# Splitting new expert weights on VectorE alone, over four points of a slot

## The chip, the cores and the metric

The kernel runs on one core of a Trainium2 chip. The metric is the device time in microseconds; several executions of one kernel are given by their median.

## The reference

Three stages follow one another on 10,112 tokens (2 sequences of 5,056) of 256 channels:

```python
h = a_t[:, t] * h + norm * sig_i * x          # gated linear scan over time, fp32
logits = x @ w_gate + modality_bias[modality_id]; e = argmax(logits)
out[e] = gate * (relu(x[e] @ w1[e]) @ w2[e])  # 8 experts, 256 -> 1024 -> 256
...                                           # and the same again, without the bias
```

The scan's output is the tokens' input of the first mixture of experts, whose output is that of the second. Only the expert with the highest logit works on a token, so which expert's weights are needed is known only at run time.

## The kernel before, in words

**Work.** The scan runs in 10 chunks of up to 512 time steps (`chunk_at`), whose rows are scattered by expert into the DRAM table X1. The experts' work is cut into slots of T = 256 tokens of one expert: 40 slots of the first layer and 40 of the second are always run (`slots`), and more, under a condition, where the tokens are spread badly. Which expert a slot has, and whether its weights differ from those that its weight set holds, a planner on VectorE works out from the counts (`plan_steps`); the engines read it into registers.

**Precision.** Each fp32 value v is split into a high part h, written by ScalarE in the type float32r, and a low part l = v - h. A product is then three TensorE products: hh, hl and lh (L911 to L913 for the first product, L925 to L927 for the second).

**A slot.** It has POINTS = 6 points. At points 0 to 3, `ffn1` does a quarter of the hidden units each: 12 products, then hTh by ScalarE (L915) and hTl by VectorE (L916). Three PSUM buffers (`ph`) hold the quarters, so TensorE can run ahead of VectorE by that much. At points 4 and 5, `ffn2` does half of the second product each (24 products); the first half needs the hidden quarters 0 and 1, the second half quarters 2 and 3. At point 3 the next slot's rows are transposed (`transposes`, xh by ScalarE, xl by VectorE). The end of a slot's work (`end_steps`: output rows by L937, L942 and L956, and in the first layer the choice of expert and the row's place for the second layer, L347 to L380 and L958 to L964, then GpSimd's scatter, L218) is spread over the points of the next slot.

**Weights.** There are two weight sets, used by slots in turn (`wset`), each of w1h, w1l, w2h and w2l. `load_weights` has SyncE fetch the next slot but one's weights in quarters of 128x1024 into `stage` buffers (five of them): part 0 is two quarters of w1, part 1 two quarters of w2. In the main loop both are put on a list at point 4 and taken from it one per point, so at points 4 and 5, if the slot's plan is due by then. `split` turns quarters of `stage` into high and low parts: `piece` has ScalarE write h (L874) and then the engine named by a letter in `by` write l (L875), V for VectorE and G for GpSimd. In the main loop the quarters 0 and 1 of the next slot are split at point 4, 2 and 3 at point 5 (`SPLIT`), with `by` = 'VVGG': the low parts of w1 on VectorE, those of w2 on GpSimd. Part 4 of `split` is a small extra piece of 128x64 in the first layer, the gate columns of the second layer's choice (`stagew`), on VectorE. The very first slot has its quarters split before the main loop, with 'VVVG'. All of it stands under a branch on the register f2 (L791), which skips it where the weights are already there. `own_gates` (L851) stands behind quarter 1 under a further branch (L855).

**Order.** Each engine runs its instructions in program order. The order is written out by hand: an agenda of ticks (`at`, `at_all`, `early`, `later`) lays the scan's steps, the planner's and the end steps between the points. GpSimd has the scatters, some copies of a few columns, and the w2 pieces. Between the layers `nest` (L1076) holds the conditional slots of the first layer behind a branch that every engine takes.

Of the kernel before, what the change touches and what calls it, by code (L numbers as in the profile page):

```python
# [29 lines left out]
CUTS = (1, 2, 3, 4, 6, 8)  # L30
SW_QUEUES = 8
POINTS = 6
SPLIT = (4, 4, 5, 5)
AHEAD = 11
T0 = 45
START = (5, 15, 34)
# [29 lines left out]
         send=32)]  # L66
LISTS = (4, 4, 4, 4, 8)
LATE = 4
BY = ('VVVG', 'VVGG', 'VVGG')
WARM = ((0, 'r', 1, 4, 2), (0, 'i', 1, 8, 2), (0, 'q', 1, 10, 3))  # L70
ALIGN = (0, 5)

# [1 line left out]
def STEP(c):  # L74
    return STEPS[min(c, len(STEPS) - 1)]
# [104 lines left out]
def scan_moe_moe2(tc, xT, rT, iT, apar, mod, mbias, wg1, wg2, wA1, wB1, wA2, cst_d, ids_d, tab_d, out):  # L180
# [11 lines left out]
    with ExitStack() as st:  # L192
# [130 lines left out]
        def run(steps):  # L323
            for f in steps:
                f()
# [67 lines left out]
        def at(tick, f, early=False):  # L393

            agenda.setdefault(tick, ([], [], []))[0 if early else 1].append(f)
# [301 lines left out]
        def fresh(pi):  # L697

            return pi == 0 or plans[pi][0] != plans[pi - 1][0]
# [2 lines left out]
        main = [(pi, s) for pi, pl in enumerate(plans) for s in range(pl[3])]  # L702
        NS = len(main)
        xT_, hT, pos = {}, {}, {}

        class Ring:

# [3 lines left out]
            def __init__(self, pool_, shape, dt, name, n):  # L711
                self.args, self.n, self.at_hand = (pool_, shape, dt, name), n, []
# [26 lines left out]
        class Slot:  # L739


            def __init__(self, pi, s, ws, pool_, bufs, tag=""):
                self.pi, self.s, self.ws, self.pool, self.bufs, self.tag = pi, s, ws, pool_, bufs, tag
                self.layer = plans[pi][0]
                self.always = not tag and s < 2 and fresh(pi)
                self.maybe = s >= plans[pi][3]
                self.v = None
                self.xpool, self.xtag = pool_, tag
                self.tiles = {}

# [28 lines left out]
        def guard(sl):  # L779

            if not sl.maybe:
                return nullcontext()
            if sl.v is None:
                sl.v = sl.entry(2, {ET.SP, ET.Activation, ET.DVE, ET.PE, ET.Pool}, 1)
            return tc.If(sl.v > 0)

        def when(slot, f, body):
            if slot.always:
                body()
            else:  # L790
                with tc.If(f > 0):  # L791
                    body()
# [9 lines left out]
        def load_weights(sl, part, gates=True):  # L802
            wA = wA1 if sl.layer == 1 else wA2
            if part == 0:
                sl.ev = sl.entry(0, {ET.SP}, E - 1)
                sl.f = None if sl.always else sl.entry(1, {ET.SP}, 1)
            js = {0: (0, 1), 1: (2, 3), 2: ()}[part]
            for j in js:
                sl.t(f"st{j}")
            gates_too = part > 0 and gates and sl.layer == 1  # L810
            if gates_too:
                sl.t("stw")

            def body():
                w = wA[bass.ds(sl.ev, 1)]
                for j in js:
                    SP.dma_start(sl.t(f"st{j}")[:], w[:, :, j * F:(j + 1) * F].rearrange("o p f -> p (o f)"))
                if gates_too:
                    SP.dma_start(sl.t("stw")[:], wg_all[:, bass.ds(sl.ev, 1)].rearrange("p o c d -> p (o c) d"))

            when(sl, sl.f, body)
# [25 lines left out]
        def first_gate(sl):  # L847
            gate(sl.gw, [sl.ring(n_).next()[:] for n_ in ("pt", "ph")], sl.t("stw"))
            SP.dma_start(wg_all[:, bass.ds(sl.ev, 1)].rearrange("p o c d -> p (o c) d"), sl.t("stw")[:])
# [15 lines left out]
                            V.tensor_reduce(out=stw[:, i * 4:i * 4 + 4, half * 4 + e], in_=t4, axis=AX.X, op=ALU.add)  # L865
                SP.dma_start(wg_all[:, bass.ds(ev, 1)].rearrange("p o c d -> p (o c) d"), stw[:])

        def split(sl, *parts, by=BY[2]):

            h1, l1, h2, l2 = wset[sl.ws]  # L870
            eng = dict(V=V, G=G)

            def piece(h, l, src, by=V):
                A.activation(h, src, func=ACTF.Copy)  # L874
                by.tensor_tensor(out=l, in0=src, in1=h.bitcast(F32), op=ALU.subtract)  # L875

            def body():
                for part in parts:
                    if part == 4:
                        continue  # L880
                    src = sl.t(f"st{part}")[:]
                    if part < 2:
                        piece(h1[:, part, :], l1[:, part, :], src, eng[by[part]])
                    else:
                        c = slice(part * 4 - 8, part * 4 - 4)
                        piece(h2[:, c, :D], l2[:, c, :D], src.rearrange("p (c d) -> p c d", d=D), eng[by[part]])
                if 1 in parts and sl.layer == 1 and not sl.always:
                    own_gates(sl)
                if 4 in parts and sl.layer == 1:
                    piece(h2[:, :, D:], l2[:, :, D:], sl.t("stw")[:])  # L890

            if 0 in parts and not sl.always:
                sl.f2 = sl.entry(1, {ET.Activation, ET.DVE, ET.Pool} | ({ET.SP} if sl.layer == 1 else set()), 1)
            when(sl, None if sl.always else sl.f2, body)

# [71 lines left out]
        slots = [Slot(pi, s, t % 2, mp, (3, 5)) for t, (pi, s) in enumerate(main)]  # L967
# [10 lines left out]
        for pi in range(1, len(plans)):  # L978
            layer, after, _, _, _, t0 = plans[pi]
            if layer == 1:  # L980
                by = slot_tick(t0 - 2, 3) - STEP(after - 1)["send"] - plan_ticks(pi)
# [34 lines left out]
        def early(upto):  # L1016

            later(upto - 1)
            if ticks[0] < upto:
                a, b, c = agenda.get(upto - 1, none)  # L1020
                run(a)
                agenda[upto - 1] = [], b, c

        def later(upto, *others):

            while ticks[0] < upto:
                a, b, c = agenda.pop(ticks[0], none)
                ticks[0] += 1
                run(a)
                for l in [f() for f in c] + list(others if ticks[0] == upto else ()):  # L1030
                    b = weave(b, l)
                run(b)
                others = others if ticks[0] < upto else ()
            for l in others:
                run(l)
# [8 lines left out]
        for sl in slots[:2]:  # L1044
            sl.ev = sl.entry(0, {ET.SP}, E - 1)
            first_gate_load(sl)
        load_weights(slots[1], 0)
        for i, tick in enumerate(FIRST):
            at(tick, lambda i=i: split(slots[0], i, by=BY[0]), early=True)
        later(T0)  # L1050
        load_weights(slots[1], 1, gates=False)
        transposes(slots[0])
# [66 lines left out]
        ends = [Slot(pi2, s, (NS + i) % 2, mp, (3, 5)) for i, s in enumerate(range(plans[pi2][3], plans[pi2][2]))]  # L1119
        line = slots + ends  # L1120
        prev = nest = None
        todo = []
        for t, sl in enumerate(slots):
            nxt, nx2 = (line[t + 1:] + [None, None])[:2]
            last1 = plans[sl.pi][0] == 1 and plans[sl.pi][4]
            a, b, c_, d, e, f = end_steps(prev)
            tick = lambda point: slot_tick(t, point) + 1
            run(a)
            if nest and sl.layer == 2:
                nest()  # L1130
                nest = None
            for point in range(POINTS):
                early(tick(point))
                if point < 4:
                    ffn1(sl, point)
                else:
                    ffn2(sl, point - 4)
                if last1 and sl.s == plans[sl.pi][3] - 2 and point == 2:
                    later(sent(NC - 1) + 1)
                    fetch, nest = maybe_steps(sl.pi)  # L1140
                    fetch()
                if t == 0 and point == 0:
                    for k in range(KD):
                        SP.dma_start(wgr[:, k, :], wg2[:, k, :].rearrange("p e -> e p"))
                if t == 0 and point in GATE:
                    first_gate(line[GATE.index(point)])
                    split(line[GATE.index(point)], 4)
                if nxt and point == 3:
                    with guard(nxt):
                        transposes(nxt)  # L1150
                if nxt:
                    parts = [i for i in range(4) if SPLIT[i] == point]
                    if parts:
                        split(nxt, *parts, *([4] if 3 in parts and t else []), by=BY[1 if t == 0 else 2])
                if nx2 and point == 4:
                    todo += [(nx2, lambda sl=nx2: (load_rows(sl), load_weights(sl, 0))), (nx2, lambda sl=nx2: load_weights(sl, 1))]
                if point == 2:
                    while todo:
                        later(listed[todo[0][0].pi] + 1)
                        todo.pop(0)[1]()  # L1160
                if todo and listed[todo[0][0].pi] < tick(point):
                    todo.pop(0)[1]()
                if point == 4:
                    run(e)
                later(tick(point), *{0: [b], 1: [c_], 2: [d], 5: [f]}.get(point, []))
            prev = sl
# [52 lines left out]
```

## Time and profile before

| | us |
|---|---|
| median of 3 executions | 1195.64 |
| lowest, highest | 1190.05, 1197.01 |
| the profiled execution's own time | 1185.72 |
| its span (first to last instruction) | 1183.9 |
| TensorE busy | 1090.3 (92%) |
| VectorE busy | 670.7 (57%) |
| ScalarE busy | 511.6 (43%) |
| GpSimd busy | 384.7 (32%) |

The rows below come from one profiled execution, and their times count from its span's start. An instruction's row gives start, duration, engine, source line, operation, output and inputs, and in brackets the idle time of its engine before it with what ended it. Engine names: PE is TensorE, DVE VectorE, ACT ScalarE, POOL GpSimd, SP SyncE; a q behind a name is the engine's sequencer. PEclk is the granted TensorE clock as a share of full speed, with 1.0 for 2.4 GHz and 0.5 for 1.2 GHz.

### The profile page before, as it was taken

Reading aid. Unit: us, or ns where it says so; the run is one execution under the profiler, and the core shown is the slowest. Engines: PE = TensorE matmul, PEld = TensorE weight load, DVE = VectorE, ACT = ScalarE, POOL = GpSimd, SP = SyncE. Lnnn points to the kernel's source line nnn. Section 1 sums busy time; section 2 is a strip of 40 time slices with the busy share of each in tenths; the row PEclk is TensorE's granted clock in tenths of the full one; section 3 lists DMA queues with packets and bytes.
Section 4 is the critical chain, followed back from the end, with each engine's and each line's share of the span. In section 5 each row is a group of like instructions: output and inputs, shape, how many; then the busy total and the mean of one; then the engine's idle time right before and its main releaser. Section 6 shows DMA issues by size and latency. Waiting matters only on the chain. (4 is left out here: it accounts for less than half of the span.)

```text
span 1183.9 us, 27134 instructions
## 1 busy us (share of the span) xinstructions
PE 1090.3 (92%) x9112; PEld 1069.1 (90%) x9112; DVE 670.7 (57%) x1945; ACT 511.6 (43%) x817; POOL 384.7 (32%) x414
## 2 busy tenths in 40 slices
PE   4287899887999999999999899999999999999997
PEld 2286899877999899999999899999999999999997
DVE  6786798768776867565456734333434443333352
ACT  7744576437263734223334323322534542224362
POOL 2425352356242514241212411311333531113152
PEclk9698999989899999999999899999999999999999
DMA  7766554355333212151115233113332431113350
GB/s 243 242 138 237 167 184 149 112 184 177 109 109 114 100 47 74 38 150 47 45 48 155 93 94 117 46 46 116 116 114 80 133 117 50 42 54 105 121 177 26
DMA packets 71305, 133.70 MB, mean 113 GB/s; under 512 B 11804, under 2 KB 39459, under 8 KB 71106
## 3 DMA queue, kind: packets, MB, share of 16 engines
q1 hardware_dynamic: 59250, 100.20, 27.9%
q0 software_dynamic: 11856, 31.25, 7.4%
q8 instruction: 76, 1.25, 0.5%
q14 instruction: 123, 1.01, 0.3%
HBM read 95.49 MB, written 37.04 MB: 112 GB/s over the span
## 5 line engine op out<-in xcount | busy, mean ns | idle before, releaser
L911 PE MATMUL ph<-xh,w1h 128*128 128x256 f32 x1312 | 376.0, 287 | 28.3 <-DVE base L377 6.5
L925 PE MATMUL po<-w2h,hTh 128*128 128x256 f32 (+1 forms) x1344 | 392.6, 292 | 4.0 <-issue 2.2
L927 PE MATMUL po<-w2h,hTl 128*128 128x256 f32 (+1 forms) x1344 | 382.3, 284 | 4.8 <-DVE hTl L916 2.5
L926 PE MATMUL po<-w2l,hTh 128*128 128x256 f32 (+1 forms) x1344 | 381.6, 284 | 3.0 <-issue 1.9
L912 PE MATMUL ph<-xl,w1h 128*128 128x256 f32 x1312 | 370.7, 283 | 4.4 <-DVE xl L902 4.4
L913 PE MATMUL ph<-xh,w1l 128*128 128x256 f32 x1312 | 371.0, 283 | 2.0 <-DVEq L855 1.0
L916 DVE SCALAR_TENSOR_TENSOR hTl<-ph,hTh 128x512 fp32r<-128x512 f32 x336 | 231.3, 688 | 235.0 <-ACT hTh L915 178.2
L915 ACT ACTIVATE hTh<-ph 128x512 fp32r<-128x512 f32 x336 | 199.2, 597 | 346.4 <-PE ph L913 283.1
L911 PEld LDWEIGHTS ph<-xh,w1h 128*128 128x128 f32 x1312 | 253.1, 193 | 31.4 <-issue 13.8
L925 PEld LDWEIGHTS po<-w2h,hTh 128*128 128x128 f32 x1344 | 255.6, 190 | 6.3 <-issue 3.7
L927 PEld LDWEIGHTS po<-w2h,hTl 128*128 128x128 f32 x1344 | 254.9, 190 | 6.9 <-DVE hTl L916 4.2
L926 PEld LDWEIGHTS po<-w2l,hTh 128*128 128x128 f32 x1344 | 255.4, 190 | 4.3 <-issue 3.0
L912 PEld LDWEIGHTS ph<-xl,w1h 128*128 128x128 f32 x1312 | 251.1, 191 | 4.6 <-DVE xl L902 4.6
L913 PEld LDWEIGHTS ph<-xh,w1l 128*128 128x128 f32 x1312 | 250.5, 191 | 2.9 <-DVEq L855 1.4
L218 POOL DMA_INDIRECT out_dram<-orow,xr x88 | 86.6, 984 | 284.1 <-ACT orow L937 237.8
L937 ACT ACTIVATE orow<-po,xr 128x256 f32<-128x256 f32 x124 | 57.7, 472 | 239.0 <-PE po L927 229.8
L218 POOL DMA_INDIRECT X<-orow,rib x80 | 80.8, 1010 | 179.7 <-DVE lgb L956 47.8
L875 POOL TENSOR_TENSOR w2l<-stage,w2h 128x1024 fp32r<-128x1024 f32 x37 | 94.2, 2566 | 132.2 <-ACT w2h L874 132.2
L942 DVE TENSOR_SCALAR orow<-po,xr 128x256 f32<-128x256 f32 x44 | 21.3, 483 | 148.7 <-PE po L927 148.7
L218 POOL DMA_INDIRECT X<-row,ria x79 | 90.1, 1141 | 24.1 <-issue 19.4
L460 PE MATMUL ps<-wI,it 128*128 128x136 f32 x280 | 49.3, 302 | 21.4 <-DVE it L439 15.6
L460 PEld LDWEIGHTS ps<-wI,it 128*128 128x128 f32 x280 | 40.0, 201 | 24.2 <-ACT rt L412 11.1
(171 smaller groups left out, 1042.1 us busy)
## 6 DMA issues: line engine op xcount, KB each, us to landing
stage<-in_wA SPq DMA_DIRECT2D x76, 512.0 KB
xr<-X SPq DMA_DIRECT2D x84, 258.0 KB
rt<-in_rT SPq DMA_DIRECT2D x18, 512.0 KB
it<-in_iT SPq DMA_DIRECT2D x18, 512.0 KB
xt<-in_xT SPq DMA_DIRECT2D x18, 512.0 KB
X<-zr SPq DMA_DIRECT2D x17, 258.0 KB
it<-in_wB SPq DMA_DIRECT2D x4, 512.0 KB
out_dram<-orow,xr POOLq DMA_INDIRECT x88
```

The lines of the kernel that those rows point to most:

```text
L218: i = G.indirect_dma_start(out=dst, out_offset=bass.IndirectOffsetOnAxis(ap=idx, axis=0), in_=rows, in_offset=None, bounds_check=bound, oo ...
L460: PE.matmul(p[:, k * (P + E):(k + 1) * (P + E)], l[:, k, :], wI[:, k, :], start=True, stop=True)
L875: by.tensor_tensor(out=l, in0=src, in1=h.bitcast(F32), op=ALU.subtract)
L911: PE.matmul(p[:, j, :], h1[:, k, cs], sl.t("xh")[:, k, :], start=k == 0, stop=False)
L912: PE.matmul(p[:, j, :], h1[:, k, cs], sl.t("xl")[:, k, :], start=False, stop=False)
L913: PE.matmul(p[:, j, :], l1[:, k, cs], sl.t("xh")[:, k, :], start=False, stop=k == KD - 1)
L915: A.activation(hh[:], p[:], func=ACTF.Relu)
L916: V.scalar_tensor_tensor(out=hl[:], in0=p[:], scalar=0.0, in1=hh[:].bitcast(F32), op0=ALU.max, op1=ALU.subtract)
L925: PE.matmul(p[h][:, :wd], hh, h2[:, c, :wd], start=c == 0, stop=False)
L926: PE.matmul(p[h][:, :wd], hh, l2[:, c, :wd], start=False, stop=False)
L927: PE.matmul(p[h][:, :wd], hl, h2[:, c, :wd], start=False, stop=c == KF - 1)
L937: A.activation(orow[:, h, :D], p[h][:, :D], func=ACTF.Copy, scale=g1[:, h:h + 1])
```

## The change

The letter sets `BY` go; `split` defaults to 'VVVV', so that in the main loop and in the conditional slots every low part is VectorE's. Only the first slot keeps 'VVVG'. The four quarters of the next slot are split at points 2, 3, 4 and 5, one each, if they were requested at least LOADED = 4 points before; otherwise at the old points. The moment of the request is kept per slot in `came`. The register f2 is read at the first `split` of a slot, whichever part that has.

```diff
-SPLIT = (4, 4, 5, 5)
+SPLIT = (2, 3, 4, 5)
+SPLIT_LATE = (4, 4, 5, 5)
+LOADED = 4
...
-BY = ('VVVG', 'VVGG', 'VVGG')
...
+        now = [-POINTS]
...
-                self.v = None
+                self.v = self.f2 = None
...
                 sl.f = None if sl.always else sl.entry(1, {ET.SP}, 1)
+                sl.came = {}
+            sl.came[part] = now[0]
...
-        def split(sl, *parts, by=BY[2]):
+        def split(sl, *parts, by='VVVV'):
...
-            if 0 in parts and not sl.always:
+            if sl.f2 is None and not sl.always:
                 sl.f2 = sl.entry(1, {ET.Activation, ET.DVE, ET.Pool} | ({ET.SP} if sl.layer == 1 else set()), 1)
...
-            at(tick, lambda i=i: split(slots[0], i, by=BY[0]), early=True)
+            at(tick, lambda i=i: split(slots[0], i, by='VVVG'), early=True)
...
+        now[0] = 0
...
             for point in range(POINTS):
+                now[0] = t * POINTS + point
...
                 if nxt:
-                    parts = [i for i in range(4) if SPLIT[i] == point]
+                    when_ = lambda i: SPLIT[i] if t * POINTS + SPLIT[i] >= nxt.came.get(i // 2, 1 << 20) + LOADED else SPLIT_LATE[i]
+                    parts = [i for i in range(4) if when_(i) == point]
                     if parts:
-                        split(nxt, *parts, *([4] if 3 in parts and t else []), by=BY[1 if t == 0 else 2])
+                        split(nxt, *parts, *([4] if 3 in parts and t else []))
```

## Rows read from the trace of the kernel before

**Rows 1.** The page's part 1: busy us (share of the span) and instructions by engine.

```profile
PE 1090.3 (92%) x9112; PEld 1069.1 (90%) x9112; DVE 670.7 (57%) x1945; ACT 511.6 (43%) x817; POOL 384.7 (32%) x414
```

**Rows 2.** Busy time by stage: two stretches.

```profile
core 0: us, PE busy (x) PEld busy (x) DVE busy (x) ACT busy (x) POOL busy (x), PEclk, DMA share, GB/s
...
149.00:255.00 106.00, 95.34 (x770) 90.98 (x769) 83.92 (x311) 57.27 (x84) 43.04 (x60) 0.95 0.49 156
...
700.00:1165.00 465.00, 465.00 (x3958) 465.00 (x3957) 178.21 (x259) 173.54 (x281) 132.44 (x101) 1.00 0.30 93
```

**Rows 3.** The timeline of TensorE: instructions behind gaps.

```profile
91.48 0.58 PE L911 MATMUL ph<-xh,w1h 128*128 128x256 f32 x1 [5.67 <-DVE db L348]
...
113.58 0.73 PE L460 MATMUL ps<-wI,it 128*128 128x136 f32 x4 [3.19 <-ACT row L470]
...
146.20 0.58 PE L911 MATMUL ph<-xh,w1h 128*128 128x256 f32 x1 [3.20 <-DVE cnt L563]
...
284.98 0.39 PE L927 MATMUL po<-w2h,hTl 128*128 128x264 f32 x1 [0.89 <-DVE hTl L916]
...
298.82 0.55 PE L911 MATMUL ph<-xh,w1h 128*128 128x256 f32 x1 [6.19 <-DVE base L377]
...
656.68 0.55 PE L911 MATMUL ph<-xh,w1h 128*128 128x256 f32 x1 [6.35 <-DVEq L1076]
```

**Rows 4.** The timelines of GpSimd and VectorE beside pieces of w2, and undisturbed.

```profile
106.86 4.98 POOL L875 TENSOR_TENSOR w2l<-stage,w2h 128x1024 fp32r<-128x1024 f32 x2 [5.79 <-ACT w2h L874]
...
109.81 2.06 DVE L379 TENSOR_TENSOR pbb<-pbb,ohb 128x16 f32<-128x16 f32 x1
...
353.98 0.17 DVE L379 TENSOR_TENSOR pbb<-pbb,ohb 128x16 f32<-128x16 f32 x1
...
83.29 2.48 DVE L586 TENSOR_TENSOR big<-av,tab 1x64 f32<-1x64 f32 x1
...
671.12 2.10 DVE L964 TENSOR_TENSOR rib<-rb,vbb 128x2 int32<-128x2 f32 x1
```

**Rows 5.** Line 875: instructions, duration in ns (least/median/most), first and last start.

```profile
L875 DVE TENSOR_TENSOR w1l<-stage,w1h x38: 1198/1220/1227, 47.1 to 1150.7; 128x1024 fp32r<-128x1024 f32 x38
L875 POOL TENSOR_TENSOR w2l<-stage,w2h x37: 2353/2552/2953, 63.4 to 1154.1; 128x1024 fp32r<-128x1024 f32 x37
```

**Rows 6.** The waits of TensorE: us in total, times, longest.

```profile
PE ph L911 <- ACTq L791: 1.7, 2, 0.9
...
PE po L926 <- DVE w2l L875: 1.0, 1, 1.0
PE ph L913 <- DVEq L855: 1.0, 2, 0.5
PE ph L913 <- DVE w1l L875: 1.0, 2, 0.8
...
PE ph L911 <- ACT w1h L874: 0.6, 1, 0.6
```

**Rows 7.** The timeline of ScalarE, and busy time by stage from 92 us.

```profile
96.57 1.06 ACT L412 ACTIVATE rt<-rt 128x1024 f32<-128x1024 f32 x1 [5.50 <-DMA rt<-in_rT]
...
92.00:104.00 12.00, 10.96 (x67) 10.07 (x66) 5.18 (x30) 6.13 (x9) 6.80 (x10) 0.78 1.02 399
```

**Rows 8.** Lines 1076 and 791, sequencers: ns (least/median/most), first and last start.

```profile
L1076 ACTq EVENT_SEMAPHORE  x2: 17/17/17, 653.1 to 653.2; - x2
L1076 DVEq EVENT_SEMAPHORE  x2: 21/21/21, 656.5 to 656.6; - x2
...
L1076 DVEq COMPARE_BRANCH  x1: 56/56/56, 653.5 to 653.5; - x1
...
L791 DVEq COMPARE_BRANCH  x188: 43/56/69, 103.7 to 1173.4; - x188
```

**Rows 9.** The timelines of VectorE and ScalarE in a slot of the second layer.

```profile
736.69 0.69 DVE L916 SCALAR_TENSOR_TENSOR hTl<-ph,hTh 128x512 fp32r<-128x512 f32 x1 [0.73 <-ACT hTh L915]
...
740.82 0.48 ACT L937 ACTIVATE orow<-po,xr 128x256 f32<-128x256 f32 x1
```

**Rows 10.** Busy time by stage, 115 to 120 us.

```profile
115.00:120.00 5.00, 5.00 (x35) 5.00 (x34) 3.48 (x16) 1.36 (x3) 1.14 (x5) 0.73 0.54 152
```

## The prediction

> **What bounds the kernel now.** I read the page's engine line first, then busy times by stage, then the gaps on TensorE one by one. TensorE is busy for 1090.3 of 1183.9 us [rows 1]. By stage it is full from 700 to 1165 us (465.00 of 465.00), where the second layer runs, and VectorE is busy there for only 38% [rows 2]. No change to the splitting can gain in that stretch; it can only lose. Between 149 and 255 us TensorE has 95.34 of 106 us and VectorE 83.92 [rows 2]: two engines near their limit, tied by a program order written out by hand. So the gain has to come out of TensorE's gaps before 700 us.
>
> The gaps have a pattern. In the first layer (and at the step to the second) the long ones come some 9 to 11 us after pieces of new weights: 5.67 us before 91.48, 3.19 before 113.58, 3.20 before 146.20, 6.19 before 298.82, 6.35 before 656.68 [rows 3]. Each time TensorE did the first two or three quarters of the next slot's first product and then ran out, because VectorE was late: the first four end on work that VectorE does or passes on, the fifth on VectorE's queue at L1076.
>
> Why is VectorE late? GpSimd's two pieces w2l<-stage take about 2.5 us each. While one of them runs, the next VectorE `tensor_tensor` with two SBUF inputs does not end before it does. At 106.86 GpSimd begins 4.98 us of pieces; VectorE's L379, which takes 0.17 us undisturbed (353.98), takes 2.06 us from 109.81, and ends (111.87) when GpSimd does (111.84) [rows 4]. Fourteen VectorE instructions are stretched so beside pieces that the change moves, two at each of seven switches; the first is at 83.29, the last at 671.12 [rows 4]. Their time over that of undisturbed ones is 4.2, 3.3, 3.0, 3.0, 4.3, 3.8 and 3.9 us by switch, 25.5 us in all. VectorE pays more for GpSimd's help than the help saves it.
>
> **The change, part by part.** *The engine.* GpSimd has 37 such pieces of 2.55 us, VectorE 38 of 1.22 us [rows 5]. One on GpSimd belongs to the first slot, whose call keeps 'VVVG'; 36 move, two at each of 18 switches: 7 up to 668 us, 11 later. VectorE gets 2 x 1.22 = 2.44 us more per switch and loses the stall. Even if nothing of the 2.44 is hidden, the first seven switches come out at 25.5 - 7 x 2.44 = 8.4 us less VectorE time.
>
> *The places.* Weights of the next slot but one are requested at points 4 and 5 of a slot; I followed the loop with its due times through all 80 slots, and none of the requests is late, so the new condition always picks (2, 3, 4, 5) and never the late set. The two w1 pieces go from point 4 to 2 and 3; the w2 pieces are then alone at 4 and 5. Per gap, the low end is the stall less 2.44, the high end the whole gap. As VectorE has idle time before the gaps (22 of 106 us in 149 to 255 [rows 2]), I take half of the 2.44 as hidden:
> - 113.58: stall 3.3, less 1.22: 2.0 (0.8 to 3.2).
> - 146.20: 3.0 less 1.22: 1.8 (0.6 to 3.2).
> - 298.82: 4.3 less 1.22: 3.1 (1.9 to 6.2).
> - 91.48: 4.2 less 1.22 is 3.0, but the piece at point 2 now stands ahead of the first slot's gate piece, for which TensorE already waits 1.0 us [rows 6]: minus 1.2; and ScalarE waits for a scan input until 96.57 whatever TensorE does, while the DMA share is 1.02 [rows 7]. I take 1.0 (-1.2 to 3.0).
> - 656.68: this gap ends when VectorE comes through the skipped branch of L1076: it reaches the branch at 653.5 and is out at 656.5. ScalarE was out at 653.1, so at most 3.3 us can go [rows 8]. The stall is 3.8, less 2.44 is 1.4; I take 1.6, since the w1 pieces start earlier (0 to 3.3).
>
> For this last term the Trainium skill (SBUF — State Buffer, "Who interferes with whom") says that whichever of VectorE with two SBUF inputs and a GpSimd instruction that reads SBUF starts first holds the shared ports for the whole instruction. It agrees with the 2.06 us, and speaks against the change too: an added 1.22 us piece could hold up a scatter before the branch; by that this term would be 0.4 and the sum 1.2 us smaller.
>
> *Waits that go.* TensorE waits five times at a slot's start for fresh w1 (1.0 + 1.0 + 0.6 us) [rows 6]; those pieces come two points earlier: 2.6 gained (0 to 2.6). Twice it waits for ScalarE's branch (1.7 us) [rows 6], which now comes earlier: 1.0 (0 to 1.7).
>
> *Costs.* The piece at point 2 stands ahead of hTl of the last quarter on VectorE, and of hTh on ScalarE with its copy. At 284.98 TensorE waits 0.89 for hTl already [rows 3]: minus 1.2 there (0 to -2.4). In the second layer hTl of the last quarter comes at 736.69 to 737.38 [rows 9]; 1.22 later is 738.6. The half product that needs it begins near 739.4: its first output is read at 740.82 [rows 9], after 12 products of 0.12 us (1090.3 / 9112 [rows 1]). It is hidden, by 0.8 us: that cover is thin. Two more branches per slot cost VectorE 0.056 us each [rows 8]; over 40 slots of the first layer 4.5 us beside an engine that is not always the bound: minus 0.7 (0 to -4.5). GpSimd's 36 x 2.55 = 92 us fall away, but only scatters stand behind them: 0.
>
> *The clock.* After the gap at 113.58 the granted clock is 0.73 in 115 to 120 [rows 10], a stretch at the 1.2 GHz level in place of 2.4: 5 x 0.27 = 1.35 us lost. Likewise after 146.20. If both gaps nearly close, 2.5 comes back (0 to 2.7).
>
> Sum: 2.0 + 1.8 + 3.1 + 1.0 + 1.6 + 2.6 + 1.0 - 1.2 - 0.7 + 2.5 = 13.7 us. The profiled execution took 1185.72 (span 1183.9 and 1.8 around it), so 1172.0 in its terms. It lies 9.9 below the median shown, 1195.64; the prediction for a median is 1195.64 - 13.7 = 1181.9, about 1182. Of itself this case may lie between 1176 and 1189.
>
> **The rivals.** *The gaps fill again.* Before 250 us something else is late next: the scan's inputs (DMA share 1.02 in 92 to 104 [rows 7]), or VectorE, at 79% between 149 and 255. Then only the later terms stay: 3.1 + 1.6 + 1.9 (three of the five w1 waits) + 1.0 - 1.2 - 0.7 = 5.7 us, 1190. For it: the order is fixed by hand, and slack gained early is easily spent. Against: every early gap here ends on VectorE's chain.
>
> *The gaps close altogether.* The whole 2.44 is hidden: 3.2 + 3.2 + 6.2 + 3.0 + 3.3 + 2.6 + 1.7 + 2.5 = 25.7, 1170. For it: VectorE is idle for a fifth of the time. Against: at 286 to 304 it is not, and the pieces come in one slot.
>
> *VectorE becomes the bound at points 2 and 3 (slower).* The two pieces ahead of hTl and xl push both back by up to 2.44 us, and TensorE waits for them inside the same slot rather than at the next: 7 x 2.44 = 17.1 lost against low ends of 0.8 + 0.6 + 1.9 + 1.4 + 2.6 = 7.3, net 9.8 slower, 1205. It decides once the second half of the second product waits over 1 us for hTl at nearly every first-layer switch. For it: the 0.89 at 284.98. Against: between the two lies half a product, some 2.9 us. The Trainium skill (Perfetto Trace Analysis, "Optimizing Scalar/DVE Operations") would lean this way, since it advises moving work off a saturated VectorE, even to GpSimd; but it adds that the two share a port, so that it may not help, which is what the 2.06 us shows.
>
> *The late places are used after all*, so that only the engine changes: the stalls go, the w1 waits stay. 13.7 - 2.6 - 1.0 + 1.2 is 11.3, 1184. The loop speaks against it.
>
> **How the numbers follow.** Forecast 0.48, refilled 0.28, closed 0.12, slower 0.10, late places 0.02. A measurement of this kernel can tell about 1%, 12 us. Of the forecast's case some 0.82 lies beyond that; with the closed gaps and half of the late places faster gets 0.39 + 0.12 + 0.01 = 0.52. Within 1%: 0.09 of the forecast's case, 0.27 of the refilled, 0.01 and 0.02 of the slower: 0.39. Slower by over 1%: the rest, 0.09 (its price is itself close to the bound, and may be larger in the second layer). The range takes in the closed gaps and the refilled ones and part of the slower case: 1168 to 1199.
>
> **What would show it.** Right: no POOL rows of L875 after the first slot's, 75 of VectorE at 1.22; no VectorE instruction of 0.2 us stretched to 2; gaps near 113, 146 and 298 under 2 us; VectorE's sum up by 44 less 25 us, near 690; 465 of 465 still in the second layer. Wrong: gaps of the same length that end on DMA or on hTh; waits on hTl inside ffn2 of over a microsecond; TensorE idle after 700 us; GpSimd pieces that stall nobody, with gaps as long without them.

## The result, and the profile after

| | before, us | after, us | ratio, 95% interval |
|---|---|---|---|
| first comparison, 4 executions each | 1195.70 | 1183.51 | 0.9897 (0.9856 to 0.9938) |
| second chip, 11 and 6 | 1171.31 | 1163.22 | 0.9935 (0.9920 to 0.9950) |
| third chip, 25 and 7 | 1188.34 | 1178.56 | 0.9904 (0.9867 to 0.9942) |

The times are medians; ratio and interval are those of the comparison and need not equal the quotient of the two medians. By the medians the change saves 12.2, 8.1 and 9.8 us; 13.7 were forecast, and 1182 as the time. The two profiled executions show almost nothing of it: 1185.72 before, 1184.67 after. The one before was 10 us under the median of its comparison, the one after 1.2 us over its own. So the traces are read here for mechanisms, and the size of the gain is taken from the medians.

The page's first part after the change (columns as in [rows 1]):

```profile
PE 1093.8 (92%) x9112; PEld 1073.6 (91%) x9112; DVE 690.7 (58%) x1981; ACT 512.9 (43%) x817; POOL 296.8 (25%) x378
```

VectorE has 36 instructions more and GpSimd 36 fewer, as said. VectorE's sum grew by 20.0 us. The 36 pieces alone would add 43.9 (36 x 1.22), so some 24 us of stretching went; 25.5 had been counted. Line 875 of before is line 879 now (columns as in [rows 5]):

```profile
L879 DVE TENSOR_TENSOR w1l<-stage,w1h x38: 1203/1219/1227, 47.3 to 1150.3; 128x1024 fp32r<-128x1024 f32 x38
L879 DVE TENSOR_TENSOR w2l<-stage,w2h x37: 1201/1217/1226, 59.8 to 1152.5; 128x1024 fp32r<-128x1024 f32 x37
L879 POOL TENSOR_TENSOR w2l<-stage,w2h x1: 2550/2550/2550, 64.4 to 64.4; 128x1024 fp32r<-128x1024 f32 x1
```

The only piece left on GpSimd is the first slot's. All 75 on VectorE take 1.22 us. The counterpart of the instruction that [rows 4] shows at 2.06 us takes 0.17, right behind the pieces, in VectorE's timeline after:

```profile
110.96 1.21 DVE L879 TENSOR_TENSOR w2l<-stage,w2h 128x1024 fp32r<-128x1024 f32 x1
...
112.51 0.17 DVE L380 TENSOR_TENSOR pbb<-pbb,ohb 128x16 f32<-128x16 f32 x1
...
293.26 1.22 DVE L879 TENSOR_TENSOR w2l<-stage,w2h 128x1024 fp32r<-128x1024 f32 x1 [1.50 <-ACT w2h L878]
294.40 1.28 DVE L440 TENSOR_TENSOR_SCAN it<-rt,carry,it 128x512 f32<-128x512 f32 x1
...
296.65 1.20 DVE L879 TENSOR_TENSOR w2l<-stage,w2h 128x1024 fp32r<-128x1024 f32 x1
297.92 1.27 DVE L440 TENSOR_TENSOR_SCAN it<-rt,carry,it 128x512 f32<-128x512 f32 x1
```

Of the 14 stretched instructions of before none is left; one that was never to go, beside the first slot's GpSimd piece, stays. TensorE's gaps, after (compare [rows 3]):

```profile
74.29 0.59 PE L930 MATMUL po<-w2l,hTh 128*128 128x264 f32 x1 [2.53 <-DVE w2l L879]
...
96.95 0.58 PE L915 MATMUL ph<-xh,w1h 128*128 128x256 f32 x1 [6.30 <-DVE hTl L920]
...
114.37 0.73 PE L461 MATMUL ps<-wI,it 128*128 128x136 f32 x4 [0.80 <-ACT row L471]
...
143.14 0.39 PE L915 MATMUL ph<-xh,w1h 128*128 128x256 f32 x1 [0.25 <-DVE cnt L564]
...
152.74 0.59 PE L931 MATMUL po<-w2h,hTl 128*128 128x264 f32 x1 [2.51 <-DVE xl L906]
...
287.58 0.39 PE L929 MATMUL po<-w2h,hTh 128*128 128x264 f32 x1 [0.98 <-ACT hTh L919]
...
299.60 0.55 PE L915 MATMUL ph<-xh,w1h 128*128 128x256 f32 x1 [4.82 <-DVE pbb L380]
...
410.83 0.35 PE L915 MATMUL ph<-xh,w1h 128*128 128x256 f32 x1 [1.32 <-DVE pbb L380]
...
655.84 0.55 PE L915 MATMUL ph<-xh,w1h 128*128 128x256 f32 x1 [4.45 <-ACTq L1080]
```

In this trace the gaps near 113 and 146 are all but gone; those near 91, 298 and 656 are not. The busy times by stage: first before, over the stretch around the two gaps that closed (columns as in [rows 2]), then after, with one stretch more ahead of it and the second layer:

```profile
104.00:116.00 12.00, 8.09 (x57) 7.45 (x56) 9.56 (x24) 6.06 (x11) 7.28 (x6) 0.93 0.15 43
116.00:134.00 18.00, 18.00 (x151) 17.95 (x151) 11.74 (x48) 6.60 (x13) 2.74 (x6) 0.95 0.77 247
134.00:149.00 15.00, 11.80 (x105) 11.54 (x104) 12.15 (x38) 10.91 (x16) 7.98 (x6) 0.87 0.19 68
```

```profile
core 0: us, PE busy (x) PEld busy (x) DVE busy (x) ACT busy (x) POOL busy (x), PEclk, DMA share, GB/s
...
92.00:104.00 12.00, 7.05 (x44) 7.06 (x44) 6.19 (x34) 5.91 (x8) 1.93 (x3) 0.72 1.04 373
...
104.00:116.00 12.00, 9.88 (x80) 9.05 (x80) 10.22 (x34) 8.15 (x15) 1.93 (x3) 1.00 0.23 80
116.00:134.00 18.00, 17.82 (x152) 17.60 (x151) 12.89 (x50) 7.50 (x15) 3.07 (x8) 1.00 0.83 268
134.00:149.00 15.00, 14.56 (x138) 14.01 (x136) 14.06 (x55) 11.96 (x17) 5.80 (x7) 1.00 0.24 66
...
700.00:1165.00 465.00, 464.90 (x3955) 464.69 (x3953) 201.76 (x282) 173.18 (x281) 83.36 (x79) 1.00 0.29 93
```

From 104 to 149 us TensorE runs 365 instructions instead of 308 (an instruction on the border of two rows is counted in both), at full clock. In the second layer it stays full although VectorE does 24 us more there.

Where along the kernel does the gain arise? All 8064 expert products are in each trace, 96 to a slot, so counting them gives the moment at which a slot begins (x.5: its second product). The profiled execution of before in us, the others as differences to it; the second traces are from e0 and e9 below, which ran on two different chips:

| slot | before | before, second trace | after | after, second trace |
|---|---|---|---|---|
| 1 | 81.5 | -0.4 | +4.8 | +3.6 |
| 2.5 | 119.8 | -2.3 | -0.4 | -2.9 |
| 4.5 | 149.6 | -2.5 | -4.6 | -7.4 |
| 8.5 | 210.4 | +1.3 | +6.1 | -0.5 |
| 13.5 | 303.5 | -2.8 | +2.1 | -4.8 |
| 40.5 | 664.3 | +1.4 | -0.3 | -5.3 |
| 83.5 | 1171.0 | +1.7 | -0.4 | -5.4 |

Both executions of the changed kernel are late at slot 1 and 5 to 7 us early at slot 4.5. Against the first trace of before they then lose 11 and 7 us up to slot 8.5; but the second trace of before loses 4 there as well, so single executions don't place the gain more finely than that. From slot 40.5 on hardly anything changes.

### The profile page after: what moved, and what is told of

Its sections match the earlier page's. It is cut to its first block, busy times and chain, and to the rows that moved or that the text cites. A ratio compares the mean times of both kernels' runs of the same rounds, so it can differ in the third digit from the quotient of the medians.

```text
span 1182.9 us, 27884 instructions
## 1 busy us (share of the span) xinstructions
PE 1093.8 (92%) x9112; PEld 1073.6 (91%) x9112; DVE 690.7 (58%) x1981; ACT 512.9 (43%) x817; POOL 296.8 (25%) x378
## 5 line engine op out<-in xcount | busy, mean ns | idle before, releaser
L931 PEld LDWEIGHTS po<-w2h,hTl 128*128 128x128 f32 x1344 | 257.8, 192 | 9.5 <-DVE hTl L920 3.8
L930 PEld LDWEIGHTS po<-w2l,hTh 128*128 128x128 f32 x1344 | 258.1, 192 | 4.1 <-DVE w2l L879 2.7
L219 POOL DMA_INDIRECT out_dram<-orow,xr x88 | 92.5, 1052 | 411.3 <-ACT orow L941 363.6
L219 POOL DMA_INDIRECT X<-row,ria x79 | 87.0, 1102 | 24.9 <-issue 20.3
L906 DVE TENSOR_TENSOR xl<-pt,xh 128x512 fp32r<-128x512 f32 x82 | 55.8, 680 | 2.0 <-ACTq L793 1.3
```

The costliest lines, as they stand in the source:

```text
L219: i = G.indirect_dma_start(out=dst, out_offset=bass.IndirectOffsetOnAxis(ap=idx, axis=0), in_=rows, in_offset=None, bounds_check=bound, oo ...
L906: V.tensor_tensor(out=sl.t("xl")[:], in0=p[:], in1=sl.t("xh")[:].bitcast(F32), op=ALU.subtract)
L930: PE.matmul(p[h][:, :wd], hh, l2[:, c, :wd], start=False, stop=False)
L931: PE.matmul(p[h][:, :wd], hl, h2[:, c, :wd], start=False, stop=c == KF - 1)
```

## The experiments

Ratios are to the kernel before, run beside each on its chip: e0 to e3 ran on one chip, e4 to e7 on another (the second of the table), e9 to e12 on a further one (the third). Diffs are to the changed kernel.

**The two kernels again.** The profile from which the forecast was worked out lies 10 us under its median, so the first question is whether it was an odd one. No edit in any of the three.

> The kernel before, unchanged, with a profile of its own. The profiled execution shown of it took 1185.72 us, 10 below its median, and the one of the changed kernel 1184.67, so the two traces differ by 1 us and the medians by 12. Theory A (the gaps behind GpSimd's pieces vary from execution to execution, and the one shown was a lucky one): the new profile lies near 1195 and has 8 to 12 us more in TensorE's gaps before 700 us, at the switches of weights. Rival B (the profile shown was ordinary and the difference lies outside it): the new profile again near 1186, with the timed executions near 1195.

1186.74 us (12 executions) beside 1187.16 (29), 0.9998 (0.9975 to 1.0022), and the profiled one at 1186.89: its trace has the same stretched instructions (15 with the first slot's, some 28 us over their undisturbed time, in both) and the same gaps, 298's smaller by 1.6 us:

```profile
111.28 0.73 PE L460 MATMUL ps<-wI,it 128*128 128x136 f32 x4 [3.22 <-ACT row L470]
...
294.96 0.55 PE L911 MATMUL ph<-xh,w1h 128*128 128x256 f32 x1 [4.60 <-DVE base L377]
...
657.66 0.55 PE L911 MATMUL ph<-xh,w1h 128*128 128x256 f32 x1 [6.95 <-DVEq L1076]
```

A time near 1186 is a usual one for the kernel before on this chip; that its usual time is 1195 was not confirmed. The 29 executions reach from 1176.72 to 1195.58.

> The changed kernel again, unchanged, beside the kernel before on the same chip. The first comparison gave 0.9897 from four executions each. If the sum of the prediction (13.7 us) is right, 0.986 to 0.991. If the engine alone is worth what its own run showed (0.9958) and the first slot costs some 5 us, as in the profile, 0.994 to 0.999.

1163.22 beside 1171.31, 0.9935 (0.9920 to 0.9950). The ratio that 13.7 us would give here, 0.9883, lies outside; the measured one lies between the two cases that were named.

> The changed kernel once more, as the measure for the other three on the same chip: 0.992 to 0.995 of before, as the last comparison gave.

1178.56 beside 1188.34, 0.9904 (0.9867 to 0.9942).

**The engine without the places.** Every low part on VectorE, at the old points.

```diff
-SPLIT = (2, 3, 4, 5)
+SPLIT = (4, 4, 5, 5)
```

> The changed kernel with the places of before (points 4, 4, 5, 5), so that only the engine differs. Theory of the stall (the pieces on GpSimd hold VectorE up): most of the gain stays, 0.988 to 0.994 of before, and no small VectorE instruction is stretched to 2 us. Rival of the places (the earlier points bring the gain): 0.997 to 1.003, with gaps as long as before behind each switch. In the first slot, where the changed profile loses 4.8 us by the first product of the second slot, the loss is gone or under 2 us.

1182.32, 0.9958 (0.9928 to 0.9989). Again on the third chip:

> The changed kernel with the old places (4, 4, 5, 5). If the engine brings the gain and the places neither bring nor cost anything in sum: the changed kernel's ratio within 0.002, 0.992 to 0.996. If the earlier places bring the waits for fresh w1 (2.6 us) and more: 0.996 to 0.998, 2 to 4 us above the changed kernel. If the early pieces cost the first slot more than they bring later: 0.988 to 0.991.

1182.50, 0.9940 (0.9907 to 0.9973). The engine alone gives 5 to 6 us, and beside a piece of w2 no instruction is stretched but the first slot's. At slot 1 the two are some 1 us late.

**The places without the engine.** w2 on GpSimd as before, at the new points.

```diff
-        def split(sl, *parts, by='VVVV'):
+        def split(sl, *parts, by='VVGG'):
```

> The changed kernel with the engines of before (VVGG) at the new points 2, 3, 4, 5. Theory of the stall: little gain, 0.996 to 1.004 of before; the fourteen stretched VectorE instructions are still there, since the w2 pieces stay on GpSimd at points 4 and 5; the waits for fresh w1 at a slot's start (2.6 us) are gone. Rival of the places: 0.988 to 0.994. In the first slot the loss of 4.8 us is there, if it comes from the piece at point 2.

1184.20, 0.9982 (0.9954 to 1.0009): not told from no change. 12 instructions are stretched, the first slot's among them, by 27.7 us in all, as much as before. The longest is the 128x64 piece of gate columns, 0.22 us undisturbed and 4.53 at 253.69; at another switch GpSimd and VectorE show:

```profile
104.03 4.72 POOL L879 TENSOR_TENSOR w2l<-stage,w2h 128x1024 fp32r<-128x1024 f32 x2
```

```profile
105.09 3.75 DVE L879 TENSOR_TENSOR w2l<-stagew,w2h 128x64 fp32r<-128x64 f32 x1
```

Both end within 0.1 us of each other (108.75 and 108.84). And yet one of the two early gaps is closed here as well, and the other, at slot 4, is 1.47 us in place of 3.20:

```profile
110.91 0.73 PE L461 MATMUL ps<-wI,it 128*128 128x136 f32 x4 [0.45 <-ACT row L471]
```

From 104 to 149 us TensorE runs 356 instructions at full clock, as in the traces of the changed kernel (352 to 366), and 359 and 357 (at 0.97 and 0.98) with the engine alone, where these two gaps are 1.3 to 1.9 us. So in this stretch either half of the change does nearly what both do, and the closing of the early gaps does not by itself show the stall at work.

Engine and places together would be 0.9958 x 0.9982 = 0.9940 if they added up; the changed kernel's three ratios do not contradict that. On one chip the engine alone (1182.32) and the places alone (1184.20) are not told apart. What the places add to the engine is left open: beside e1 the changed kernel with the first slot late (e3, below) is 4.7 us faster, beside e10 the three kernels with new places are faster by 3.9, 1.0 and not at all.

**The suspected cost by itself.** To the changed kernel, GpSimd gets useless work per w2 quarter of about the old piece's length: once differences that read SBUF, once memsets that only write it (with one copy of two columns, so that they start at the same moment).

```diff
+        extra = wp.tile([P, 2, D], BF16, name="extra", bufs=1)
+        G.memset(extra[:], 0.0)
...
+                        if by == 'VVVV':
+                            for i in range(2):
+                                x2 = h2[:, part * 4 - 8 + 2 * i:part * 4 - 6 + 2 * i, :D].bitcast(F32)
+                                G.tensor_tensor(out=extra[:], in0=x2, in1=x2, op=ALU.subtract)
```

> The changed kernel, and GpSimd also computes two useless differences of 128x512 from each new high quarter of w2, into a tile of its own that nobody reads. No result of GpSimd is waited for by VectorE, ScalarE or TensorE. Theory of the stall (an instruction of GpSimd that reads SBUF holds up VectorE's with two SBUF inputs): VectorE instructions of 0.2 us and of 1.2 us beside them are stretched again, and the time is 3 to 8 us above the changed kernel's. Rival (in the kernel before VectorE waited for GpSimd's results through the order of the writes of w2l): nothing is stretched and the time is that of the changed kernel within 1.5 us.

```diff
+        extra = wp.tile([P, D], F32, name="extra", bufs=1)
+        G.memset(extra[:], 0.0)
...
+                        if by == 'VVVV':
+                            G.tensor_copy(extra[:, :2], h2[:, part * 4 - 8, :2].bitcast(F32))
+                            for _ in range(8):
+                                G.memset(extra[:], 0.0)
```

> As the run with useless reads, but GpSimd, after one small copy of two columns of the high quarter, writes zeros into its own tile for a like time (eight of 128x256 per quarter, some 2 to 3 us). Theory of the stall through reading: nothing is stretched, and the time is that of the changed kernel within 2 us. Rival (any work of GpSimd holds VectorE up): the same stretching as with reads.

With the reads 1180.07, 1.0072 (1.0058 to 1.0086): 16.9 us over the changed kernel on the same chip and slower than before; 3 to 8 had been expected, so the price was twice the most that was thought of. With the writes 1162.11, 0.9921 (0.9908 to 0.9934), 1.1 us under the changed kernel with overlapping intervals: no cost. The costliest lines of GpSimd (busy us, mean ns, then idle time before), reads first:

```profile
L896 POOL TENSOR_TENSOR extra<-w2h 128x512 bf16<-128x512 f32 x72 | 111.3, 1546 | 93.8 <-ACT w2h L880 89.6
```

```profile
L896 POOL MEMSET extra<- 128x256 f32 x288 | 89.9, 312 | 16.6
...
L894 POOL COPY extra<-w2h 128x2 f32<-128x2 f32 x36 | 17.3, 481 | 86.6 <-ACT w2h L880 85.0 <-ACT xh L911 0.6
```

111.3 us of reads against 89.9 + 17.3 = 107.2 us of writes with their copies: GpSimd's time is nearly the same, what it touches differs. VectorE's timeline in the same place, reads first:

```profile
250.89 2.26 DVE L881 TENSOR_TENSOR w2l<-stage,w2h 128x1024 fp32r<-128x1024 f32 x1
...
256.31 0.86 DVE L380 TENSOR_TENSOR pbb<-pbb,ohb 128x16 f32<-128x16 f32 x1
```

```profile
247.53 1.22 DVE L881 TENSOR_TENSOR w2l<-stage,w2h 128x1024 fp32r<-128x1024 f32 x1
...
249.09 0.17 DVE L380 TENSOR_TENSOR pbb<-pbb,ohb 128x16 f32<-128x16 f32 x1
```

With the reads 48 VectorE instructions more are stretched by over 0.3 us. Before 700 us these are 26, by 19.1 us together, nine of them VectorE's own new pieces; after it they are 22, all new pieces, under a TensorE that stays full. With the writes none more is stretched. That a memset is short (0.31 us) does not hide it: 68 VectorE `tensor_tensor` with both inputs in SBUF run while one is under way, and none is over 0.06 us longer than usual. With the reads two of TensorE's old gaps are back:

```profile
112.49 1.28 PE L463 MATMUL ps<-wI,it 128*128 128x136 f32 x4 [3.07 <-ACT row L473]
...
650.28 0.55 PE L921 MATMUL ph<-xh,w1h 128*128 128x256 f32 x1 [7.38 <-DVEq L1086]
```

The gap near 298 is not: it is the same with the reads, shown first, and with the writes.

```profile
289.07 0.36 PE L921 MATMUL ph<-xh,w1h 128*128 128x256 f32 x1 [4.52 <-DVE base L378]
```

```profile
281.17 0.55 PE L921 MATMUL ph<-xh,w1h 128*128 128x256 f32 x1 [4.51 <-DVE base L378]
```

The Trainium skill (SBUF — State Buffer, "Who interferes with whom") says that a VectorE instruction with two SBUF inputs contends with a GpSimd instruction that reads SBUF and not with one that only writes it. The pair of runs agrees, at a price of 17 us of 1163. The reads also cost more than the whole change brought: VectorE now has the pieces of its own besides, and most of those (31 of 36) are stretched too. So 17 us is the price in this kernel and not that of the stall in the kernel before.

**The places varied.** At slot 1 the changed kernel is 4.8 us late. First with the old points for the switch in the first slot alone:

```diff
-                    when_ = lambda i: SPLIT[i] if t * POINTS + SPLIT[i] >= ...
+                    when_ = lambda i: SPLIT[i] if t and t * POINTS + SPLIT[i] >= ...
```

> The changed kernel, but during the very first slot the old places (4, 4, 5, 5). Theory F (the early pieces cost the first slot: they stand ahead of its hTl, xl and gate piece on VectorE): the waits before 59.98 and 74.29 us go back to 4.4 and 1.0, and the time is 2 to 4 us below the changed kernel's 1183.5, if nothing later takes it back. Rival: the waits come back elsewhere before 150 us (a scan input lands when it lands), and the time is that of the changed kernel within 1.5 us.

1177.59, 0.9909 (0.9879 to 0.9938). The first wait is shorter than after, and 4.58 lies within what three traces of the changed kernel show there (6.30, 3.48, 3.45); the wait before 59.98, which was to go back to 4.4, is 4.94 before 60.31:

```profile
73.47 0.39 PE L930 MATMUL po<-w2l,hTh 128*128 128x264 f32 x1 [0.99 <-DVE w2l L879]
...
91.70 0.54 PE L915 MATMUL ph<-xh,w1h 128*128 128x256 f32 x1 [4.58 <-DVE hTl L920]
```

The changed kernel was not among the four of that chip, so it was run beside it again:

> The changed kernel with the old places in the first slot. If the loss of the first slot (1.5 us more wait for the gate piece, in both profiles of the changed kernel) stays to the end: 1 to 4 us below the changed kernel, 0.989 to 0.992. If it is taken back before 120 us by a scan input that lands when it lands: the same as the changed kernel within 1 us.

1181.48, 0.9922 (0.9887 to 0.9958), against 0.9904 of the changed kernel beside it. The wait that it shortens is not worth anything that can be measured: by slot 2.5 the changed kernel had caught up anyway.

The same edit, and the first pieces at point 3 rather than 2 (only the second edit is shown):

```diff
-SPLIT = (2, 3, 4, 5)
+SPLIT = (3, 3, 4, 5)
```

> The changed kernel with the old places in the first slot and (3, 3, 4, 5) in the others, so that no piece stands ahead of hTl of the last quarter and of xl. Theory (the piece at point 2 costs the waits on hTl in the second product, 1.6 us near 282 and 1.0 near 148 in the run with the first slot late): 1 to 3 us below that run, near 0.989 of before. Rival (the pieces cost the same wherever they stand, since VectorE's queue is full up to the next slot): the same as that run, 0.991, the waits on hTl inside the second product gone and the gap at the next slot longer by as much.

1163.08, 0.9931 (0.9916 to 0.9945), beside 0.9935: the same. In the two traces of this chip the wait for hTl is smaller (0.69 at 269.78, against 1.66), and the gap near 298 larger (5.30 before 280.38, against 2.91), as the rival said. But a third-chip trace of the changed kernel has 0.7 and 6.25 at these places, so one trace each does not show that the one is traded for the other.

The first slot late, and its own last quarter on VectorE as well, so that GpSimd has no piece left (only the second edit is shown):

```diff
-            at(tick, lambda i=i: split(slots[0], i, by='VVVG'), early=True)
+            at(tick, lambda i=i: split(slots[0], i), early=True)
```

> The run with the first slot late, and the first slot's own last quarter on VectorE too, so that GpSimd has no piece at all. The one stretched VectorE instruction that is left (2.9 in place of 0.7 us, at 63 us) goes, and the piece costs VectorE 1.2 us there. If that chain (VectorE up to the gate piece, some 72 us) reaches the end: 0.5 to 1.5 us below the run beside it. If not: the same.

1182.56, 0.9933 (0.9901 to 0.9964). No instruction is stretched beside a piece of weights any more, and the time is that of the others.

## Why the prediction was right, point by point

**The mechanism** was right in its cause: GpSimd's pieces stretched VectorE, and with them gone the kernel is faster at the old places too (0.9958, 0.9940). Useless reads bring stretching and a loss (e5), writes of the same length do not (e6). How much of the gain it makes up is less sure. Where both ran on one chip, the engine alone gave 5.8 us and the whole change 9.8, with overlapping intervals. The second layer was neutral, as said.

**The size** was somewhat too large: 13.7 against 8.1 to 12.2. The second chip's interval excludes it, the other two (7 to 17 us) do not. That 1182 came so near the first comparison's 1183.5 is in part luck: that comparison shows the largest of the three gains, and the terms do not come out as they were added up. The stated range, 1168 to 1199, also had the time before in it. By terms, in two traces of before (the first, e0) and three of after (the first, e9, e4):

- 113.58: 2.0 forecast. 3.19 and 3.22 before, 0.79 to 0.80 after, so 2.4. A new wait of 0.6 for VectorE stands 5 us ahead of it in all three. The earlier places close this gap as well (e2).
- 146.20: 1.8 forecast, 3.20 less 0.25 is 3.0; but 2.5 of it came back 9 us later in this trace, as a wait put down to xl before 152.74, and 2.51 in the third chip's trace too. In the second chip's it is 0.5. VectorE itself sits idle for 1.24 before 151.22 there; why is not shown.
- 298.82: 3.1 forecast, 6.19 less 4.82 is 1.4 in the first pair. This step failed. Before it is 6.19 and 4.60, after 4.82, 6.25 and 2.91, and it is 4.5 both with the useless reads and with the writes, so no gain can be told. I had put the gap down to the stall. The two scans of 1.28 stood there before as well; what is new in the last stretch of VectorE are both w2 pieces (2.44), and a wait of 1.50 for ScalarE's copy (the rows from 293.26 above; 1.46 in the third chip's trace, none in the second's, where the gap is 2.91). Together they nearly take back the stall of 4.3. ScalarE has no idle time there; its timeline after:

```profile
289.92 1.28 ACT L413 ACT_TABLE_LOAD   x1
291.22 1.06 ACT L413 ACTIVATE rt<-rt 128x1024 f32<-128x1024 f32 x1
292.18 1.04 ACT L878 ACTIVATE w2h<-stage 128x1024 fp32r<-128x1024 f32 x1
```

- 91.48: 1.0 forecast, 5.67 less 6.30 is a loss of 0.6 in the first pair; the other traces of after have 3.48 and 3.45, a gain of 2.2. All lie within its bounds (-1.2 to 3.0). The loss that I named (the piece at point 2 ahead of the first slot's gate piece) is about the 1.2 counted: the wait for w2l before 74.29 went from 1.0 [rows 6] and 1.5 to 2.5. The wait for xl before 59.98 grew by some 0.5 besides. Neither costs anything in the end that e11 could measure.
- 656.68: 1.6 forecast, 6.35 less 4.45 is 1.9. Here the stall does show: the four traces with reads on GpSimd (before, e0, e2, e5) have 6.4 to 7.4, the other ten 4.5 to 6.2. Unlike the other gaps this one stands ahead of the slot's first product and not after two or three quarters of it, as the prediction had read it. And ScalarE's exit does not stay at 653.1, as the bound of 3.3 assumed; it and VectorE's come together. The two scatters at the branch (653.07 and 654.35) take 0.98 us each, as before, so the hold-up of a scatter that was feared did not come. The sequencers at the branch, after (columns as in [rows 8]):

```profile
L1080 DVEq EVENT_SEMAPHORE  x2: 21/21/21, 655.7 to 655.8; - x2
L1080 ACTq EVENT_SEMAPHORE  x2: 17/17/17, 655.8 to 655.8; - x2
...
L1080 ACTq COMPARE_BRANCH  x1: 45/45/45, 651.4 to 651.4; - x1
L1080 DVEq COMPARE_BRANCH  x1: 56/56/56, 652.8 to 652.8; - x1
```

- The waits for fresh w1: 2.6 forecast, and they are gone (two of the five, 1.0 us, were put down to the branch L855 and not to w1). The waits for ScalarE's branch: 1.0 forecast, and they are gone too, but waits for VectorE stand in their slots (1.32 before 410.83). This term was 0.
- hTl: -1.2 forecast. The wait near 285 is there, of 1.2, 0.7 and 1.7 in the three traces of the changed kernel, partly for hTh (287.58); before it was 0.9 [rows 3] and 0.6. So about 0.5 was lost, at most 1.0.
- The clock: 2.5 forecast. Over 104 to 149 the granted clock rose from 0.93, 0.95 and 0.87 to 1.00, worth 12 x 0.07 + 18 x 0.05 + 15 x 0.13 = 3.7. In the other traces of after it is 1.00 there as well. But over 54 to 92, in the first slot with its longer waits, it fell from 0.89 and 0.91 to 0.82 in all traces of after, 38 x 0.07 = 2.7 given back, and in the first also from 0.78 [rows 7] to 0.72 over 92 to 104. Over 149 to 255 it is 0.95 and 0.97 before and 0.93 and 0.95 in the first and the third chip's trace of after, 106 x 0.02 = 2.1 more. So the term was right where it was put, and in sum nothing is left of it in either pair.

Together the gaps of TensorE between 50 and 700 us (added up from its timeline, without those put down to "issue") come to 49.2 and 48.9 us in the two traces of before, and to 44.9 and 40.8 in the first and third comparison's traces of after. The last leaves out 3.48 us that are put down to "issue" before 92.94, where the other two traces of after wait for hTl; with them it is 44.3. So 4 to 5 us went, where the forecast's terms without the clock and the branches (13.7 - 2.5 + 0.7) made it 11.9. These pairs of profiled executions differ by 1.0 and 6.9 us; what the medians gained beyond that stands in no trace and stays open.

**The rivals.** *The gaps fill again* (1190) is what happened to the terms at 298.82, at 91.48 and of ScalarE's branch, but early terms held as well; its 5.7 us lies under all three gains by the medians, and near the 4 to 5 us of the gaps. *Closed altogether* is out: 4.8 and 4.5 us gaps remain. *VectorE as the bound at points 2 and 3* did not come at nearly every switch, as it would have had to: in three traces of the changed kernel no wait for hTl inside the second product is over 1.7 (one is over 1), and e7 with fewer pieces ahead of hTl is no faster. The Trainium skill (Perfetto Trace Analysis, "Optimizing Scalar/DVE Operations"), which leaned to it, advises GpSimd for relief and adds that the shared port may spoil it; e5 agrees with that caveat, at 17 us. *The late places* are not what ran, though e1 and e10 show that they would have given about half of the gain.

## What to carry to other kernels

A helper engine's time is not what its help costs: look beside each of its instructions for instructions of the other engine that take longer than elsewhere (short ones end when the helper's does), and add up their excess. Here 25.5 us on VectorE bought 17 us of relief (14 pieces x 1.22). And before a change of 1% is read from two traces, run both kernels again: single profiled executions stood 1 us apart where the medians stood 12 apart. A gap that closes counts only if TensorE does not wait as long 10 us later, and only if a second trace of before does not have it smaller already (6.19 and 4.60 here).

## What had not been expected of the hardware

The kernel before takes 1171 us on one chip and 1187 to 1196 in the other comparisons, a difference larger than the change. In the traces of the four kernels of the fast chip TensorE has no gap put down to "issue" over 0.16 us between 50 and 700 us; in all others these gaps add up to 5 to 11 us, at changing places, like this one of the changed kernel:

```profile
250.08 0.28 PE L930 MATMUL po<-w2l,hTh 128*128 128x264 f32 x1 [0.83 <-issue]
```

What TensorE waits for there was not tried and stays open. Over 240 to 262 us, where the first trace of before has eight of them, its granted clock is 0.84; over the same stretch of the changed kernel's trace on the fast chip, where none stands, it is 1.00.

At the branch around the conditional slots, which every engine skips, VectorE takes 2.9 us (652.8 to 655.7) and ScalarE 4.3 from the comparison to the next event; over the 14 traces it is 2.9 to 4.7 and 2.6 to 5.8. TensorE's gap there is under 4.45 us in none of them. How much of that is the branch's own and how much a wait for other engines was not separated.
